# A fixed, hand-made order on all engines for a fused linear-attention and feed-forward kernel, with the v casts on GpSimd

## Chip, cores, metric

One core of a Trainium2 chip. The metric is the device time of one execution in microseconds (us). Span means the stretch that the profile covers; timed runs are about 2 us longer.

## The reference, cut to what matters

```python
# q, k, v: (8 batches, 8 heads, 576 positions, 64)
def phi(x): return np.where(x > 0, x, np.exp(x) - 1.0) + 1.0
q_p, k_p = phi(q), phi(k)
kv  = einsum('bhsd,bhse->bhde', k_p, v);  z = k_p.sum(axis=2)
num = einsum('bhsd,bhde->bhse', q_p, kv)
den = einsum('bhsd,bhd->bhs', q_p, z)[..., None] + 1e-6
x   = (num / den).transpose(0, 2, 1, 3).reshape(4608, 512)
out = (((x @ w1) * (x @ w2)) @ w3) @ w_out       # d_ff 1024
```

## The kernel before

w3 and w_out are fused on the chip into one weight (wf). The tokens are cut into nine chunks of 512 columns. Chunk c needs the attention of batches 0 to c. For each chunk TensorE (PE) runs eight feed-forward groups (F), each of four a_ps and four b_ps matmuls, and four output groups (O). ScalarE (ACT) copies a_ps out of PSUM, where the matmul results stand (its evacuation), VectorE (DVE) multiplies it by b_ps. The attention of a later batch runs beside it: phi of k and q on ACT and DVE, kv, transposes of q (tr), num and den (nd), a logarithm and exponential on ACT as reciprocal, a product on DVE.

Only the weight loads have a fixed order. For all else the framework's scheduler chooses each engine's order; then each engine works its queue in that order and stops at the first instruction that must wait (ScalarE stood so for 14.9 us, as the prediction shows).

```python
def phi_steps(name, b, dst_j, dst_r):
    def ex(j0):
        nc.scalar.activation(out=ev[...], in_=xv[...], func=AF.Exp)
        nc.vector.tensor_scalar_min(out=ev[...], in0=ev[...], scalar1=1.0)
    def st(j):                       # max(x + 1, e): two SBUF inputs
        nc.vector.scalar_tensor_tensor(out=dst_j[...], in0=xv[...], scalar=1.0,
                                       in1=ev[...], op0=ALU.add, op1=ALU.max)
...
def f_unit(c, f):
    a_ps = mm_ps.tile(...); b_ps = mm_ps.tile(...)      # 4 PSUM banks in this pool
    for ps, w in ((a_ps, w1_sb), (b_ps, w2_sb)):
        for kc in range(KC):
            nc.tensor.matmul(ps, w[:, kc, ...], xt[:, kc, cs], ...)
    a_sb = sm.tile(...)
    nc.scalar.copy(out=a_sb, in_=a_ps)
    nc.vector.tensor_mul(out=abs_[c][:, f, :], in0=a_sb, in1=b_ps)
...
k1 = load_qkv("k", k, 1)
after(k1, wl[11])                    # k of batch 1 behind the second w3 block
...                                  # q, v of batch 1; attention of batch 0
for f in range(FC):
    f_unit(0, f)
for i in range(FC):
    wf_unit(i)                       # 8 transposes of w3, copy on ACT, 8 matmuls
run(k_steps(1) + q_steps(1) + v_steps(1))
```

Of the kernel before, what the change touches and what calls it, by code (L numbers as in the profile page):

```python
# [8 lines left out]
F32 = mybir.dt.float32  # L9
BF16 = mybir.dt.bfloat16  # L10
AF = mybir.ActivationFunctionType
ALU = mybir.AluOpType

P = 128
NCH = 512
# [3 lines left out]
def kernel(  # L19
# [11 lines left out]
    nc = tc.nc  # L31
    B, H, S, D = q.shape
# [3 lines left out]
    KC = DM // P  # L36
    FC = DFF // P
    NJ = 4
# [75 lines left out]
    def phi_steps(name, b, dst_j, dst_r):  # L114
        x = raw[name, b]
        e = e_p.tile([P, JW + RW], BF16, tag="e", name="e")
        xv = x[:, 0:JW].rearrange("p (h j d) -> p h j d", h=H, j=NJ)
        ev = e[:, 0:JW].rearrange("p (h j d) -> p h j d", h=H, j=NJ)

        def ex(j0):  # L120
            nc.scalar.activation(out=ev[:, :, j0:j0 + 2, :], in_=xv[:, :, j0:j0 + 2, :], func=AF.Exp)  # L121
            nc.vector.tensor_scalar_min(  # L122
                out=ev[:, :, j0:j0 + 2, :], in0=ev[:, :, j0:j0 + 2, :], scalar1=1.0)

        def exr():
            nc.scalar.activation(out=e[:, JW:], in_=x[:, JW:], func=AF.Exp)
            nc.vector.tensor_scalar_min(out=e[:, JW:], in0=e[:, JW:], scalar1=1.0)

        def st(j):
            nc.vector.scalar_tensor_tensor(  # L130
                out=dst_j[:, j, :].rearrange("p (h d) -> p h d", h=H),
                in0=xv[:, :, j, :], scalar=1.0, in1=ev[:, :, j, :], op0=ALU.add, op1=ALU.max)

        def sr():
            nc.vector.scalar_tensor_tensor(
                out=dst_r, in0=x[:, JW:], scalar=1.0, in1=e[:, JW:],
                op0=ALU.add, op1=ALU.max)

        return [lambda: ex(0), lambda: (st(0), st(1)), lambda: ex(2), lambda: (st(2), st(3)),
                exr, sr]  # L140

    ph = {}

# [9 lines left out]
        ph["q", b] = (qj, qr)  # L153
        return phi_steps("q", b, qj, qr)

    def v_steps(b):
        x = raw["v", b]

        def cj(j0):
            (nc.scalar.copy if b == 0 and j0 == 0 else nc.vector.tensor_copy)(  # L160
                out=vt[:, j0:j0 + 2, :, 0:D],
                in_=x[:, 0:JW].rearrange("p (h j d) -> p j h d", h=H, j=NJ)[:, j0:j0 + 2])

        def cr():
            nc.vector.tensor_copy(
                out=vr[:, :, 0:D], in_=x[:, JW:].rearrange("p (h d) -> p h d", d=D))

        return [lambda: cj(0), lambda: (cj(2), cr())]


    kvz, qts = {}, {}

    def kv_unit(b):
        kj, kr = ph["k", b]
        t = att.tile([P, KC, 2, P], BF16, tag="kvz", name="kvz")
        for g in range(2):
            kvp = at_ps.tile([P, 2, 256], F32, tag="at", name="kvp")
            for hp in (2 * g, 2 * g + 1):
                o = kvp[:, hp % 2, 0:2 * (D + 1)]
# [16 lines left out]
            nc.vector.tensor_tensor(  # L196
                out=tg[:, :, 1, :].rearrange("p a (h e) -> p a h e", h=2),
                in0=src[:, :, :, D:D + 1].to_broadcast([P, 2, 2, D]), in1=mask, op=ALU.mult)
        kvz[b] = t

    def tr_unit(b, part):
        qj, qr = ph["q", b]
        if part == 0:
            qts[b] = att.tile([P, KC, S], BF16, tag="qt", name="qt", bufs=1)
        qt = qts[b]
        if part < 2:
            tp = at_ps.tile([P, KC, 2, P], BF16, tag="at", name="tp")
            for jj in range(2):
                for hp in range(KC):
                    nc.tensor.transpose(  # L210
                        tp[:, hp, jj, :], qj[:, 2 * part + jj, hp * P:(hp + 1) * P], ident)
            nc.vector.tensor_copy(
                out=qt[:, :, part * 256:(part + 1) * 256],
                in_=tp.rearrange("p a j t -> p a (j t)"))
        else:
            for hh in range(2):
                tp = at_ps.tile([P, 2, R], BF16, tag="at", name="tp")
                rows = slice(hh * R, (hh + 1) * R)
                for i in range(2):
                    nc.tensor.transpose(  # L220
                        tp[:, i, :], qr[rows, i * P:(i + 1) * P], ident[rows, rows])
                nc.vector.tensor_copy(out=qt[:, 2 * hh:2 * hh + 2, NJ * P:S], in_=tp)

    def nd_finish(n_ap, d_ap, dst, shape):
        r = lr.tile(shape, F32, tag="lr", name="r")
# [23 lines left out]

    abs_ = {}  # L250

    def f_unit(c, f):
        if f == 0:
            abs_[c] = ab_p.tile([P, FC, NCH], BF16, tag="ab", name="ab")
        cs = slice(c * NCH, (c + 1) * NCH)
        a_ps = mm_ps.tile([P, NCH], F32, tag="mm", name="a_ps")
        b_ps = mm_ps.tile([P, NCH], F32, tag="mm", name="b_ps")
        for ps, w in ((a_ps, w1_sb), (b_ps, w2_sb)):
            for kc in range(KC):
                nc.tensor.matmul(ps, w[:, kc, f * P:(f + 1) * P], xt[:, kc, cs],  # L260
                                 start=(kc == 0), stop=(kc == KC - 1))
        a_sb = sm.tile([P, NCH], F32, tag="a_sb", name="a_sb")
        nc.scalar.copy(out=a_sb, in_=a_ps)  # L263
        nc.vector.tensor_mul(out=abs_[c][:, f, :], in0=a_sb, in1=b_ps)  # L264

    def o_unit(c, m):
        ab = abs_[c]
# [37 lines left out]
        return nc.gpsimd.dma_start(out=t, in_=moe_w3[i * P:(i + 1) * P, :])  # L305


    def wf_unit(i):
        w3b = raw["w3", i]
        tp = at_ps.tile([P, FC, P], BF16, tag="at", name="w3p")  # L310
        for kc in range(FC):
            nc.tensor.transpose(tp[:, kc, :], w3b[:, kc * P:(kc + 1) * P], ident)
        w3t = setup.tile([P, FC, P], BF16, tag="w3t", name="w3t")
        nc.scalar.copy(out=w3t, in_=tp)  # L314
        ps = mm_ps.tile([P, DM], F32, tag="mm", name="wf_ps")
        for kc in range(FC):
            nc.tensor.matmul(ps, w3t[:, kc, :], wo_sb[:, kc, :],  # L317
                             start=(kc == 0), stop=(kc == FC - 1))
        nc.scalar.copy(out=wf_sb[:, i, :], in_=ps)


    def run(steps):
        for s in steps:
            s()

    k0 = load_qkv("k", k, 0)
    q0 = load_qkv("q", q, 0)
    v0 = load_qkv("v", v, 0)
    with tc.manual_schedule(engines={mybir.EngineType.Pool}):
        wl = [i for x in range(4) for i in load_w12(x)]  # L330
        after(wl[0], q0)
        wl += [load_wo(0), load_wo(1)]
        wl += [load_w3(i) for i in range(FC)]
    k1 = load_qkv("k", k, 1)
    after(k1, wl[11])
    load_qkv("q", q, 1)
    load_qkv("v", v, 1)

    run(k_steps(0))
    run(q_steps(0))  # L340
    for p in range(3):
        tr_unit(0, p)
    run(v_steps(0))
    kv_unit(0)
    for hp in range(KC):
        nd_unit(0, hp)
    ndr_unit(0)
    for f in range(FC):
        f_unit(0, f)
    for i in range(FC):  # L350
        wf_unit(i)
    run(k_steps(1) + q_steps(1) + v_steps(1))

    for c in range(1, n_chunks + 1):
        a = c if c == 1 else c + 1
        last = c == n_chunks
        units = []
        if c == 1:
            kv_unit(1)
            for p in range(3):  # L360
                tr_unit(1, p)
            for m in range(4):
                o_unit(0, m)
                nd_unit(1, m)
            ndr_unit(1)
            for n, s in (("k", k), ("v", v), ("q", q)):
                load_qkv(n, s, 2)
            run(k_steps(2) + v_steps(2) + q_steps(2))
        if last:
            for m in range(4):  # L370
                o_unit(c - 1, m)
            break
        a = c + 1
        has = a < B
        if has and a + 1 < B:
            for n, s in (("k", k), ("v", v), ("q", q)):
                load_qkv(n, s, a + 1)
        F = lambda f: (lambda: f_unit(c, f))
        O = lambda m: (lambda: o_unit(c - 1, m)) if c > 1 else (lambda: None)
        KV = lambda: kv_unit(a)  # L380
        T = lambda p: (lambda: tr_unit(a, p))
        N = lambda h: (lambda: nd_unit(a, h))
        NR = lambda: ndr_unit(a)
        if has:
            units = [F(0), KV, F(1), O(0), T(0), T(1), F(2), T(2), O(1), F(3), N(0), F(4), N(1),
                     O(2), F(5), N(2), F(6), N(3), NR, O(3), F(7)]
        else:
            units = [F(0), F(1), O(0), F(2), O(1), F(3), F(4), O(2), F(5), F(6), O(3), F(7)]
        pq = []
        started = 0  # L390
        for i, u in enumerate(units):
            u()
            if has and a + 1 < B:
                if i == 7:
                    pq = k_steps(a + 1) + v_steps(a + 1) + q_steps(a + 1)
                if i >= 7:
                    run(pq[:2] if i > 7 else pq[:1])
                    del pq[:2 if i > 7 else 1]
        run(pq)


# [1 line left out]
_INS = ['q', 'k', 'v', 'moe_w1', 'moe_w2', 'moe_w3', 'moe_w_out']  # L403
# [26 lines left out]
```

## Time and profile before

| | before |
|---|---|
| median time, us | 288.58 (288.14 to 289.36, 3 runs) |
| span of the profiled run | 286.6 |
| last feed-forward group of chunk 0 ends | 53.77 |
| first group of chunk 2 ends | 106.58 |
| last output copy starts | 282.76 |

The rows are moments from the timeline of PE and ACT. The prediction shows the views themselves.

### The profile page before, as it was taken

How to read it: one execution, taken by the hardware profiler on the slowest of the kernel's cores; microseconds unless marked ns; L12 is line 12 of the kernel's file. 1: busy time of each engine (PE TensorE's matmuls, PEld its weight loads, DVE VectorE, ACT ScalarE, POOL GpSimd, SP SyncE). 2: the span in 40 equal slices, each digit the busy share in tenths (PEclk: the TensorE clock that was granted, in tenths of full speed). 3: DMA queues.
4: the chain of work that ended last, by engine and by line, in shares of the span. 5: the costliest groups of instructions: out<-in, count | busy, mean ns of one | idle time of the engine just before them, and what ended most of it. 6: DMA issues, size and time to landing. Idle time of an engine off the chain costs nothing.

```text
span 286.6 us, 3958 instructions
## 1 busy us (share of the span) xinstructions
PE 251.3 (88%) x1413; PEld 122.1 (43%) x1440; DVE 164.4 (57%) x327; ACT 155.2 (54%) x254; POOL 13.6 (5%) x30
## 2 busy tenths in 40 slices
PE   0188605999989999999999999999999999999994
PEld 0043201555535445445544544554455444444441
DVE  0875106913968999965985896498443442221210
ACT  3528007499693992893587279426723763333322
POOL 2472100000000000000000000000000000000000
PEclk9999965999999999999999999999999999999999
DMA  6999999992469881893496081010011111100223
GB/s 209 328 177 202 210 270 352 368 355 79 147 185 279 248 272 27 233 278 116 130 304 210 1 231 46 37 38 37 37 39 54 53 40 40 73 37 37 75 60 123
DMA packets 49715, 43.25 MB, mean 151 GB/s; under 512 B 14368, under 2 KB 44064, under 8 KB 49696
## 3 DMA queue, kind: packets, MB, share of 16 engines
q1 hardware_dynamic: 43264, 37.76, 41.7%
q0 software_dynamic: 6432, 5.24, 11.7%
q8 instruction: 11, 0.18, 0.3%
q14 instruction: 8, 0.07, 0.1%
HBM read 38.80 MB, written 9.44 MB: 168 GB/s over the span
## 4 chain that ended last, share of the span: by engine, by line
PE 72%; DMA 14%; ACT 7%; issue 3%; DVE 2%; POOL 1%; SPq 1%; another core or an unknown queue 0%; ACTq 0%; DVEq 0%
PE a_ps L260 20%; PE b_ps L260 19%; PE o_ps L270 18%; DMA w3b<-in_moe_w_dram 4%; DMA k<-in_k_dram 4%; PE wf_ps L317 4%; PE kvp L181 3%; DMA q<-in_q_dram 3%; DMA w_sb<-in_moe_w_dram 3%; PE tp L210 2%; ACT e L121 2%; PE den L234 2%; PE num L234 2%; PE kvp L187 1%; ACT o_sb L273 1%
## 5 line engine op out<-in xcount | busy, mean ns | idle before, releaser
L260 PEld LDWEIGHTS <-w_sb 128*128 128x128 bf16 x576 | 55.8, 99 | 80.3 <-issue 17.6
L260 PE MATMUL a_ps<-xt,w_sb 128*128 128x512 bf16 x283 | 75.7, 385 | 13.3 <-ACT a_sb L263 12.8
L264 DVE TENSOR_TENSOR ab<-a_sb,b_ps 128x512 bf16<-128x512 f32 x72 | 49.3, 686 | 51.9 <-PE b_ps L260 51.0
L260 PE MATMUL b_ps<-xt,w_sb 128*128 128x512 bf16 x279 | 75.1, 383 | 0.5
L270 PE MATMUL o_ps<-wf_sb,ab 128*128 128x512 bf16 x278 | 65.9, 379 | 0.4
L263 ACT COPY a_sb<-a_ps 128x512 f32<-128x512 f32 x72 | 41.8, 582 | 45.1 <-PE a_ps L260 43.8
L273 ACT COPY o_sb<-o_ps 128x512 f32<-128x512 f32 x36 | 21.1, 585 | 41.9 <-PE o_ps L270 41.4
L270 PEld LDWEIGHTS <-ab 128*128 128x128 bf16 x288 | 27.3, 98 | 31.7
L122 DVE TENSOR_SCALAR e<-e 128x1024 bf16<-128x1024 bf16 x32 | 13.2, 423 | 36.0 <-ACT e L121 35.8
L228 DVE TENSOR_TENSOR xt<-num,r 128x512 bf16<-128x512 f32 (+1 forms) x40 | 24.6, 635 | 15.3 <-ACT r L227 14.8
L226 ACT ACTIVATE r<-den,eps 128x512 f32<-128x512 f32 (+1 forms) x40 | 25.0, 646 | 11.9 <-PE den L234 11.2
L121 ACT ACTIVATE e<-k 128x1024 bf16<-128x1024 f32 x16 | 16.5, 1055 | 20.7 <-DMA k<-in_k_dram 19.1
L227 ACT ACTIVATE r<-r 128x512 f32<-128x512 f32 (+1 forms) x40 | 22.4, 586 | 0.5
L210 PE MATMUL tp<-ident,qj 128*128 128x128 bf16 x128 | 10.1, 230 | 13.6 <-DVE qj L130 13.4
L130 DVE SCALAR_TENSOR_TENSOR kj<-k,e 128x512 bf16<-128x512 f32 x32 | 20.6, 685 | 0.1
L130 DVE SCALAR_TENSOR_TENSOR qj<-q,e 128x512 bf16<-128x512 f32 x32 | 20.4, 685 | 0.0
L121 ACT ACTIVATE e<-q 128x1024 bf16<-128x1024 f32 x16 | 16.6, 1054 | 2.3 <-DMA q<-in_q_dram 2.2
L210 PEld LDWEIGHTS <-qj 128*128 128x128 bf16 x128 | 8.3, 102 | 16.1 <-DVE qj L130 14.2
L317 PE MATMUL wf_ps<-wo_sb,w3t 128*128 128x512 bf16 x61 | 14.2, 380 | 0.7 <-ACT w3t L314 0.5
L181 PE MATMUL kvp<-vt,kj 128*128 128x130 bf16 x128 | 13.9, 232 | 0.9 <-DVE vt L160 0.5
L234 PE MATMUL den<-qt,kvz 128*128 128x512 bf16 x32 | 12.9, 402 | 0.7 <-DVE xt L228 0.7
L234 PE MATMUL num<-qt,kvz 128*128 128x512 bf16 x32 | 12.8, 401 | 0.0
(42 smaller groups left out, 135.0 us busy)
## 6 DMA issues: line engine op xcount, KB each, us to landing
k<-in_k_dram SPq DMA_DIRECT2D x8, 1024.0 KB, 6.8
q<-in_q_dram SPq DMA_DIRECT2D x8, 1024.0 KB, 6.9
v<-in_v_dram SPq DMA_DIRECT2D x8, 1024.0 KB, 7.8
out_dram<-o_sb SPq DMA_DIRECT2D x32, 256.0 KB, 2.3
w_sb<-in_moe_w_dram POOLq DMA_DIRECT2D x8, 256.0 KB, 7.4
w3b<-in_moe_w_dram POOLq DMA_DIRECT2D x8, 256.0 KB, 13.0
k<-in_k_dram SPq DMA_DIRECT2D x16, 64.0 KB, 5.1
q<-in_q_dram SPq DMA_DIRECT2D x16, 64.0 KB, 6.1
```

Source lines behind the costliest of these rows:

```text
L121: nc.scalar.activation(out=ev[:, :, j0:j0 + 2, :], in_=xv[:, :, j0:j0 + 2, :], func=AF.Exp)
L130: nc.vector.scalar_tensor_tensor(out=dst_j[:, j, :].rearrange("p (h d) -> p h d", h=H), in0=xv[:, :, j, :], scalar=1.0, in1=ev[:, :, j, :] ...
L210: nc.tensor.transpose(tp[:, hp, jj, :], qj[:, 2 * part + jj, hp * P:(hp + 1) * P], ident)
L226: nc.scalar.activation(out=r, in_=d_ap, func=AF.Ln, bias=eps[:, 0:1])
L228: nc.vector.tensor_tensor(out=dst, in0=n_ap, in1=r, op=ALU.mult)
L234: nc.tensor.matmul(nd[i], t[:, hp, i, :], qt[:, hp, 0:NJ * P], start=True, stop=True)
L260: nc.tensor.matmul(ps, w[:, kc, f * P:(f + 1) * P], xt[:, kc, cs], start=(kc == 0), stop=(kc == KC - 1))
L263: nc.scalar.copy(out=a_sb, in_=a_ps)
L264: nc.vector.tensor_mul(out=abs_[c][:, f, :], in0=a_sb, in1=b_ps)
L270: nc.tensor.matmul(o_ps, ab[:, f, m * P:(m + 1) * P], wf_sb[:, f, :], start=(f == 0), stop=(f == FC - 1))
L273: nc.scalar.copy(out=o_sb, in_=o_ps)
L317: nc.tensor.matmul(ps, w3t[:, kc, :], wo_sb[:, kc, :], start=(kc == 0), stop=(kc == FC - 1))
```

## The change

The intent: all engines in program order, written so that each feed-forward group carries a share of phi and attention of later batches. Not in the cut: half of the v cast of batch 1 goes to ACT, and w3t gets a third buffer. Core of the diff, cut:

```diff
+        cast = nc.vector.tensor_copy if b == 0 else nc.gpsimd.tensor_copy      # v_unit
...
+        copy = nc.scalar.copy if b == 2 else nc.vector.tensor_copy             # tr_unit
...
-        nc.scalar.copy(out=wf_sb[:, i, :], in_=ps)
+        nc.vector.tensor_copy(out=wf_sb[:, i, :], in_=ps)
...
+    ctx.enter_context(tc.manual_schedule())
...
+    nd_unit(0, 0)
+    nd_unit(0, 1)
+    first = [f_open(0, 0), f_open(0, 1)]
+    for kc in range(KC):
+        for f in range(2):
+            f_mm(0, f, first[f][0], w1_sb, kc)
+            f_mm(0, f, first[f][1], w2_sb, kc)
+        if kc < 2:
+            nd_unit(0, kc + 2)
+        elif kc == 2:
+            ndr_unit(0)
...
+    for f in range(2, FC):
+        if f >= 6:
+            w3_tr(f - 6)
         f_unit(0, f)
...
     for i in range(FC):
+        if i + 2 < FC:
+            w3_tr(i + 2)
+        if i == 2:
+            run(ks, "e0 s0 s1")
+        elif i == 3:
+            run(ks, "e2 s2 s3 eR sR")
...                                  # q in 4 and 5, v in 6
+        wf_mm(i)
...
+        F(0)                        # chunk c, a = c + 1
+        run(qs, "s2 s3 eR sR")
+        K("e0");  kv_unit(a, (0,));  F(1)
+        K("e2");  kv_unit(a, (1,));  O(0)
+        v_unit(a + 1)
+        K("s0 s1 eR");  tr_unit(a, 0);  F(2)
...
```

## The prediction

> **What bounds the kernel now.** I began with the page: TensorE's busy tenths, the granted clock and the DMA share, side by side over the 40 slices of 7.2 us.
>
> ```profile
> PE   0188605999989999999999999999999999999994
> DVE  0875106913968999965985896498443442221210
> ACT  3528007499693992893587279426723763333322
> PEclk9999965999999999999999999999999999999999
> DMA  6999999992469881893496081010011111100223
> ```
>
> From slice 13 on PE has a 9 everywhere. Before that there is a hole in slices 4 to 6, in which the vector and scalar engines are empty too, the clock falls to 6 and 5 tenths, and DMA stays at 9. So there are two regimes. The skill warns that a busy PE is not a PE at its peak, so I then took the busy time by stretches, cut at events that the timeline shows.
>
> ```profile
> 28.10:33.50 5.40, 5.38 (x25) 2.34 (x24) 1.97 (x3) 1.03 (x2) 1.06 (x2) 1.00 1.17 211
> 33.50:46.25 12.75, 0.00 (x1) 0.00 (x0) 0.46 (x2) 1.58 (x3) 0.00 (x0) 0.65 1.10 285
> 46.25:53.77 7.52, 7.30 (x23) 2.90 (x24) 7.52 (x15) 5.35 (x8) 0.00 (x0) 0.68 1.08 349
> 53.77:88.31 34.54, 32.36 (x241) 17.98 (x244) 20.26 (x46) 28.07 (x42) 0.00 (x0) 1.00 0.70 223
> 88.31:106.58 18.27, 18.17 (x102) 8.58 (x102) 18.02 (x38) 13.72 (x23) 0.00 (x0) 1.00 0.83 249
> 106.58:282.80 176.22, 175.05 (x958) 84.21 (x975) 101.08 (x194) 91.37 (x158) 0.00 (x0) 1.00 0.30 95
> ```
>
> The columns are stretch, length, busy us (count) of PE, weight load, DVE, ACT and POOL, then clock, DMA share, GB/s. The timeline shows that a group of four 512-column matmuls starts every 0.86 us when dense: 0.216 us each at clock 1.00. The last stretch runs at that pace: it can't be shortened by an order of instructions. Nothing runs on PE between 33.50 and 46.25, and the next stretch runs three feed-forward groups (24 matmuls, 5.2 us of dense work) in 7.52 us at clock 0.68. Who held PE up, I read from the waits between 30 and 50 us:
>
> ```profile
> DVE e L122 <- ACT e L121: 14.9, 1, 14.9
> ACT e L121 <- DMA k<-in_k_dram: 14.9, 1, 14.9
> PE a_ps L260 <- ACT a_sb L263: 12.8, 1, 12.8
> ```
>
> and from the chain that ended last:
>
> ```profile
> 20.77 12.66 DMA w3b<-in_moe_w_dram
> 33.45 11.20 DMA k<-in_k_dram
> ...
> 44.67 0.02 ACT e L121
> ...
> 45.63 0.57 ACT a_sb L263
> 46.21 0.04 issue
> 46.25 1.86 PE a_ps L260 x4
> ```
>
> This is one inversion in a queue that is served in order. The scheduler put the exponential of k of batch 1 on ScalarE ahead of the evacuation of a finished a_ps. That k is held back on purpose behind the second w3 block, is issued at 33.45 and lands at 44.65. The ready evacuation stands behind it, PE has no free PSUM bank among the four, and feed-forward groups 5, 6 and 7 of chunk 0, whose inputs all lie in SBUF, wait for a transfer that they don't need.
>
> **What the Trainium skill says.** (1) "TensorE: Matmul & The Clock Gate", Part 1, says that an idle TensorE falls to half its clock after some 3.4 us and needs as much busy time to get it back. The trace agrees: after the hole the matmuls stand 0.43 us apart, not 0.216, until about 51 us. (2) "SBUF — State Buffer", Who interferes with whom, says that a GpSimd instruction that reads SBUF and a VectorE instruction with two SBUF inputs, or in a two-port mode, block each other for the whole instruction. The trace before can't show it, GpSimd does only memsets there. (3) "GPSIMD Engine Reference", section 3.1, gives 769 ns for 512 elements in a good one-input loop. From this I estimate 1.5 us for a cast of 1024 columns; no row of this trace has one. (4) "Perfetto Trace Analysis", Optimizing Scalar/DVE Operations, says that a profiled latency overlaps with the next instruction. The trace agrees: four of the 128x512 combines on DVE (685 ns each by the groups) take 2.49 us in a row, so about 0.60 us apart. I count DVE by spacing: 0.60 for 512 columns from PSUM or mixed, 0.34 for the 1024-column minimum, 0.34 for kvz.
>
> **The change part by part.**
>
> *The hole.* With every queue in program order, all eight a_sb copies of chunk 0 and the w3 copies 0 to 4 come before k of batch 1 on ScalarE. Groups 0 to 4 of chunk 0 finish by about 33.5 now; in the new order groups 0 and 1 close at about 28.4 (their inputs take the same path: num and den, logarithm, exponential, product), then six groups of 1.73 us and two blocks of w3 transposes of 0.45 follow: 28.4 + 10.4 + 0.9 = 39.7 us. Before, they ended at 53.77, without these two transposes. So 14.1 us, which are the 12.75 of the hole, 2.3 of low clock (7.52 - 5.2), less 0.9 for transposes done early, give or take 0.1. The blocks of w3 that this needs are there: issued at 19.4 and 20.8, the first by its median of 13 us near 32.4, the second at 33.4 by the chain.
>
> *Does the wait come back?* k of batch 1 still lands near 44.7, q near 47.8 (issued 33.87, longest landing 13.9), v near 50. The fused-weight loop runs from 39.7 for 8 x (1.73 + 0.45), less the two transposes done, plus 1.06 for the q transposes: to about 57.3. Its iteration 2, at about 44, is where ScalarE first asks for k: it waits perhaps nothing, and PE has two fused blocks of slack there, as w3 copies run two ahead. phi of k and q on DVE: per batch 8 x 0.60 + 4 x 0.34 + about 0.9 = 7.1 us, beside 8 fused evacuations at 0.60 newly on DVE, 4.8. I walked both queues: DVE ends this at about 58.9, one to two us behind PE, which the four PSUM banks hold up. No stall over 1 us.
>
> *Until chunk 1 ends.* From 57.3: kv 1.96, four output groups 6.9, four num/den pairs 1.73, the remainder 0.67, makes 11.3; the single num/den slots cost about 1 us in my walk: chunk 1 starts near 69.6. Chunk 1 has 13.8 + 1.96 + 1.06 + 1.73 + 0.67 = 19.2 of PE work without any output group, while DVE has about 17.5 to 18 plus waits for the logarithm and exponential; with 1 to 1.5 us of stalls it ends near 90.3 to 90.7. Before, the same work was done at 106.58. So 16 us, of which 14.1 is the hole and about 2 the 34.54 us stretch (PE busy 32.36).
>
> *Steady stretch.* PE per chunk: 96 x 0.216 + 8 x 0.216 + 1.96 + 1.06 + 0.67 = 26.1 by my sum; the dense trace has 25.8. DVE by spacing: ab 4.8, phi 7.1, kvz 1.4, qt 1.5, xt 2.7 = 17.5. ScalarE, spaced by the same reading (0.48 for an evacuation, 0.96 for an exponential): about 16. Both fit beside 25.8. The v cast that leaves DVE was 2 x 0.60 + 0.2 = 1.4 us, off the path, so it gives nothing directly. Its cost is the lock: cast on GpSimd, 2 x 1.5 + 0.4 = 3.4 us per batch, just when DVE makes k's combine (two SBUF inputs). From F(0) to the first num/den, 9.95 us of PE time, DVE must get through some 9.7 us before qt is complete. Little slack, so the lock shows as 0 to 1 us per chunk, on chunks 2 to 6: I take 0.5, 2.5 us in all. The rest (176.2 us) is as before.
>
> **Sum.** 90.5 + 176.2 + 2.5 + 3.8 (the last copy and output, as before 282.8 to 286.6) = 273.0 of span. Timed runs exceed the span by 2.0 (288.58 - 286.6): 275.0. I put down **274.5 us**, as the middle stretch may have one stall less: a gain of 14.1, 4.9%.
>
> **The rivals.** *The wait moves instead of going.* DMA share is about 1.1 from 28 to 54 us, so the loads are bound there, and k, q, v of batch 1 come no earlier. If ScalarE stands for q or v in the fused loop, copies of w3 stand behind it. For it: the queue is still in order. Against: 17 us of PE work that needs none of it now lies before their use. It would give back 4 to 7 us: 279 to 282. *VectorE becomes the bound.* Page and stretch show DVE busy 18.02 of 18.27 in chunk 1, and a fixed order can't step around a late operand. With the lock at its worst, 1 to 1.5 us in six chunks, and the middle stretch late by 2: 280 to 282. *Everything fits.* PE dense from 28.4 on: 10.4 + 3.6 + 13.8 + 1.06 + 11.3 + 19.2 = 59.4, so 87.8; + 176.2 + 3.8 + 2 = 269.8. *Nothing is gained*, because PE is 88% busy: refuted by the hole, which has no busy PE and no need.
>
> **Range and chances.** 270 to 281: from all fits to one rival in full. Slower than 282.8 would need both the moved wait and the lock. Faster by over 2%: 0.94, within 2%: 0.05, slower: 0.01.
>
> **What would show each step right or wrong.** In the new profile: no PE gap over 2 us from 28 to 90 and clock tenths of 9 there, else the first step fails. The last feed-forward matmul of chunk 0 near 40 us, chunk 1's first near 70 and last near 90. If ScalarE waits for DMA of k, q or v over 2 us while PE idles, the first rival holds. If rows of num/den or tp wait on DVE qt or kj in each chunk, and DVE's combine or minimum is longer than 685 and 423 ns beside GpSimd's casts, the second holds. The cast row itself should read near 1.5 us; at 3 or more the steady stretch loses more. I would be wrong altogether if chunk period on PE rose from 25.8 to over 27.

## The result, and the profile after

Ratios here are the mean time of one kernel's fast runs over that of the other's in the same rounds, so not quite the ratio of the medians quoted.

| | before | after |
|---|---|---|
| median, us | 288.36 | 279.73 (279.05 to 280.77, 4 runs) |
| ratio | | 0.9705 (0.9657 to 0.9753) |
| span | 286.6 | 277.9 |
| groups 0 and 1 of chunk 0 done (start of group 2) | 28.1 | 32.1 |
| last group of chunk 0 done | 53.77 | 43.37, two w3 transpose blocks (0.9 us) done as well |
| first matmul of chunk 1 | 88.31, kv and 7 transposes of the next batch done as well | 75.55 |
| first group of chunk 2 done | 106.58 | 98.09 |
| last output copy starts | 282.76 | 274.06 |

The predicted 274.5 was too low by 5.2 us; the measured time lies inside the range. The gain is 8.6 us where 14.1 was expected. The page's 40 slices after:

```profile
PE   0078899989798999999999999999999999999994
DVE  0773533795898787759666966786574442232210
PEclk9999999999999999999999999999999999999999
DMA  7999999999189935675455663011001200111122
```

The hole of slices 4 to 6 is gone, in PE and in the clock. In its place are shallow dips up to slice 12. The busy time by stretch (length, PE, weight load, DVE, ACT, POOL, clock, DMA share, GB/s), cut at the moments of the table:

```profile
28.10:43.37 15.27, 14.34 (x84) 6.91 (x83) 6.31 (x10) 8.52 (x14) 1.06 (x2) 1.00 1.13 237
43.37:75.55 32.18, 28.68 (x199) 15.45 (x201) 23.34 (x46) 21.25 (x30) 3.95 (x5) 1.00 0.88 284
75.55:98.09 22.54, 20.84 (x125) 10.47 (x128) 18.61 (x37) 19.10 (x33) 4.01 (x3) 1.00 0.91 277
98.09:274.10 176.01, 174.88 (x958) 84.57 (x975) 100.48 (x189) 95.20 (x162) 12.08 (x12) 1.00 0.32 100
```

The last stretch is 176.01 us against 176.22 before: nothing won and nothing lost. What PE waited for between 28 and 100 us (us in total, times, longest):

```profile
PE num L240 <- DVE xt L234: 1.5, 2, 1.2
PE a_ps L264 <- DVE xt L234: 1.5, 2, 0.9
PE kvp L187 <- DVE qt L218: 1.3, 1, 1.3
PE den L240 <- ACT qt L218: 0.9, 1, 0.9
```

One wait of 12.8 us has become several of about 1 us, mostly on DVE. And PE's timeline in the head, as I call all that comes before group 2 of chunk 0 (start, duration, operation):

```profile
24.16 0.58 PE L264 MATMUL a_ps<-xt,w_sb 128*128 128x512 bf16 x1 [0.94 <-DVE xt L234]
24.54 0.63 PE L264 MATMUL b_ps<-xt,w_sb 128*128 128x512 bf16 x1
24.97 0.63 PE L264 MATMUL a_ps<-xt,w_sb 128*128 128x512 bf16 x1
...
28.38 0.52 PE L240 MATMUL den<-qt,kvz 128*128 128x512 bf16 x1
28.74 0.38 PE L240 MATMUL num<-qt,kvz 128*128 128x512 bf16 x1
28.96 0.38 PE L264 MATMUL a_ps<-xt,w_sb 128*128 128x512 bf16 x1
```

Up to 28.4 the matmuls stand 0.43 us apart, then 0.22: half speed until then, although the clock row reads 9 for these slices. In the kernel before, the last matmul at that pace starts at about 22 us. The head of this trace also began its kv matmuls 0.8 us later than in the kernel before (17.04 against 16.28), so not all of the delay is clock.

### The profile page after: what moved, and what is told of

The parts are those of the page before. It is cut to its first block, busy times and chain, and to the rows that moved or that the text cites. A ratio compares the mean times of both kernels' runs of the same rounds, so it can differ in the third digit from the quotient of the medians.

```text
span 277.9 us, 3982 instructions
## 1 busy us (share of the span) xinstructions
PE 250.3 (90%) x1413; PEld 122.7 (44%) x1440; DVE 162.2 (58%) x310; ACT 155.4 (56%) x251; POOL 33.8 (12%) x50
## 3 DMA queue, kind: packets, MB, share of 16 engines
q0 software_dynamic: 6432, 5.24, 12.1%
## 4 chain that ended last, share of the span: by engine, by line
PE 75%; DMA 10%; ACT 4%; DVE 4%; POOL 3%; issue 2%; SPq 2%; ACTq 0%; DVEq 0%
PE o_ps L283 21%; PE a_ps L264 21%; PE b_ps L264 21%; DMA w3b<-in_moe_w_dram 5%; DMA q<-in_q_dram 3%; PE kvp L187 3%; POOL w_sb L306 2%; DMA k<-in_k_dram 2%; PE tp L216 2%; PE num L240 2%; PE den L240 2%; SPq L106 2%; PE kvp L193 1%; DVE wf_sb L337 1%; ACT r L232 1%
## 5 line engine op out<-in xcount | busy, mean ns | idle before, releaser
L264 PE MATMUL a_ps<-xt,w_sb 128*128 128x512 bf16 x270 | 74.6, 383 | 3.6 <-DVE xt L234 2.4
L283 PE MATMUL o_ps<-wf_sb,ab 128*128 128x512 bf16 x286 | 67.2, 379 | 0.2 <-issue 0.2
L234 DVE TENSOR_TENSOR xt<-num,r 128x512 bf16<-128x512 f32 (+1 forms) x40 | 25.5, 638 | 29.5 <-ACT r L233 29.3
L162 POOL CAST vt<-v 128x1024 bf16<-128x1024 f32 x13 | 15.6, 1228 | 130.5 <-PE kvp L187 91.8
L232 ACT ACTIVATE r<-den,eps 128x512 f32<-128x512 f32 (+1 forms) x40 | 25.8, 645 | 9.5 <-PE den L240 9.4
L233 ACT ACTIVATE r<-r 128x512 f32<-128x512 f32 (+1 forms) x40 | 23.5, 587 | 1.3
L216 PE MATMUL tp<-ident,qj 128*128 128x128 bf16 x128 | 11.0, 230 | 13.9 <-DVE qj L131 13.9
L123 DVE TENSOR_SCALAR e<-e 128x1024 bf16<-128x1024 bf16 x32 | 14.7, 461 | 14.2 <-ACT e L121 14.2
L131 DVE SCALAR_TENSOR_TENSOR kj<-k,e 128x512 bf16<-128x512 f32 x32 | 22.5, 732 | 0.2
L131 DVE SCALAR_TENSOR_TENSOR qj<-q,e 128x512 bf16<-128x512 f32 x32 | 21.0, 685 | 0.2
```

What stands on the lines that cost most here:

```text
L131: nc.vector.scalar_tensor_tensor(out=dst_j[:, j, :].rearrange("p (h d) -> p h d", h=H), in0=xv[:, :, j, :], scalar=1.0, in1=ev[:, :, j, :] ...
L216: nc.tensor.transpose(tp[:, hp, jj, :], qj[:, 2 * part + jj, hp * P:(hp + 1) * P], ident)
L232: nc.scalar.activation(out=r, in_=d_ap, func=AF.Ln, bias=eps[:, 0:1])
L233: nc.scalar.activation(out=r, in_=r, func=AF.Exp, scale=-1.0)
L234: nc.vector.tensor_tensor(out=dst, in0=n_ap, in1=r, op=ALU.mult)
L264: nc.tensor.matmul(ps, w[:, kc, f * P:(f + 1) * P], xt[:, kc, c * NCH:(c + 1) * NCH], start=(kc == 0), stop=(kc == KC - 1))
```

## The experiments

Ten runs were made, in three sets, each set with the kernel before in the same rounds. All gave correct results. Two questions: is the inversion the whole cause of the gain, and where did the rest of the expected gain go?

### Only the inversion taken away

The kernel before, scheduler and all, with a scheduling dependency (no semaphore) added by the helper that it already has:

```diff
-            nc.scalar.activation(out=ev[...], in_=xv[...], func=AF.Exp)
+            ins = nc.scalar.activation(out=ev[...], in_=xv[...], func=AF.Exp)
+            if b == 1:
+                after(ins, hold[0])
```

In a_late, hold[0] is the last a_ps copy of chunk 0; in a_late2, the fourth w3 copy.

> The kernel before, automatic order kept, with one scheduling dependency more: the exponentials of batch 1 come on ScalarE after the last a_ps evacuation of chunk 0. Theory (the one inversion on ScalarE is the whole gain, and the hand-made order adds nothing, rather gives some back): the PE hole of 12.8 us and the low clock after it go, but the exponential of k now stands in front of the third w3 copy and waits there for k, which lands near 45: 275 to 278 us. Rival (the gain of the change comes from the new order as a whole, the greedy order finds another wait of the same length elsewhere): 285 us or more.

> As the run before, but the exponentials of batch 1 come after the fourth w3 copy of the fused-weight loop, by when k has landed. Theory: 273 to 276 us, faster than the hand-made order (279.7), no PE gap over 2 us between 24 and 88 us, chunk 0's last group done near 39 us. Rival: 279 us or more, because work is only pushed to a later stretch where VectorE is full.

Measured: a_late 282.21 us, ratio 0.9799 (0.9765 to 0.9834); a_late2 280.51, ratio 0.9733 (0.9673 to 0.9793). Both are slower than the theory said, and a_late2 falls into the rival's range. Its profile says why. The chain that ended last, from 33 to 60 us, and one row of DVE's timeline:

```profile
46.20 5.23 DMA v<-in_v_dram
...
51.64 0.69 DVE vt L163
52.33 0.60 DVE ab L267
52.93 0.04 issue
52.98 5.70 PE wf_ps L322 x16
```

```profile
51.03 1.30 DVE L163 CAST vt<-v 128x1024 bf16<-128x1024 f32 x2 [13.31 <-DMA v<-in_v_dram]
```

The scheduler had put the v cast of batch 1 on DVE ahead of the product (ab) of the last group. DVE stood 13.3 us for v, PE lost 6.0 us and then ran at a low clock. It is the same kind of inversion in a second queue, but not one that the first had covered: in the kernel before, the cast stands behind that product.

```profile
54.04 0.69 DVE L264 TENSOR_TENSOR ab<-a_sb,b_ps 128x512 bf16<-128x512 f32 x1
55.59 1.29 DVE L160 CAST vt<-v 128x1024 bf16<-128x1024 f32 x2
```

The scheduler made it when the exponentials were held back. (a_late lost 5.7 us to a w3 copy behind the waiting exponential, as expected; its DVE stood for v too, 12.2 us.) So a third version, a_late3, also puts the v casts of batch 1 behind the last combine of q:

```diff
+            if b == 1:
+                after(ins, qlast[0])        # at the three v casts
```

> As a_late2 (exponentials of batch 1 after the fourth w3 copy), and also the v casts of batch 1 on VectorE after the last combine of q of batch 1. In a_late2 the greedy order had put a v cast, whose load lands at 51 us, in front of the product of group 7: PE lost 6.0 us there and ran at low clock after it. Theory (the inversions in the queues are the whole loss, and the greedy order is otherwise as good or better than the hand-made one): 272 to 275 us, 5 to 7 us under the changed kernel. Rival (freed here, the time is lost to VectorE later): 278 us or more.

Measured: 276.84 us (275.88 to 278.36), ratio 0.9593 (0.955 to 0.9637). That is short of the theory's 272 to 275, but clearly faster than the changed kernel, whose ratio in a second set below is 0.9684 (0.9664 to 0.9704). Busy time by stretch:

```profile
28.10:38.50 10.40, 10.35 (x49) 4.71 (x49) 4.72 (x7) 3.96 (x7) 1.06 (x2) 1.00 1.14 209
38.50:75.04 36.54, 32.85 (x241) 18.14 (x243) 24.38 (x53) 30.00 (x45) 0.00 (x0) 1.00 0.99 318
```

Chunk 0's last group ends at 38.50: 15.3 us earlier than before. From there to the end of chunk 2's first group (93.75) it takes 55.25 us where the kernel before took 52.81: 2.4 us are given back, 1.6 of them in one wait of a fused-weight matmul for a w3 copy. The rest is kept: the span is 274.1.

### The inversion put back alone

The changed kernel, with the first exponential of k of batch 1 moved up, and with it the minimum that follows it on DVE (both are in step e0; the rest of the edit only makes the steps earlier):

```diff
     for f in range(2, FC):
+        if f == 3:
+            run(ks, "e0")
         if f >= 6:
```

> The changed kernel with the inversion put back alone: the first exponential of k of batch 1 goes to ScalarE just before the a_ps evacuation of group 3 of chunk 0. Theory: PE stops with its four PSUM banks full near 36 to 37 us and until k lands near 45, a hole of 8 to 9 us, then low clock for about 2 us: 289 to 291 us against 279.7. Rival (the inversion is not what cost the time in the kernel before): 280 to 282 us.

Measured: 290.13 us (289.6 to 291.6), ratio 1.0079 (1.0038 to 1.0121). The waits between 30 and 50 us are of the same kind as in the kernel before, up to 3 us shorter:

```profile
DVE e L123 <- ACT e L121: 12.0, 1, 12.0
ACT e L121 <- DMA k<-in_k_dram: 12.0, 1, 12.0
PE a_ps L264 <- ACT a_sb L269: 9.9, 1, 9.9
```

One exponential and its minimum, too early in their queues, cost about 10 us, more than the whole change gains. In the kernel before, too, the minimum stood ahead of ready products on DVE; whether one of the two queues alone would do the harm was not tested. With a_late3 this settles the first question: the gain is the inversion; the rest of the hand-made order, taken as a whole, adds nothing to it.

### The v casts back on VectorE

```diff
-        cast = nc.vector.tensor_copy if b == 0 else nc.gpsimd.tensor_copy
+        cast = nc.vector.tensor_copy
```

> The changed kernel with the v casts of batches 1 to 7 back on VectorE (the first half of batch 1 stays on ScalarE). My prediction charged the GpSimd casts 2.5 us for the shared lock; the trace of the changed kernel shows no PE stall in the steady stretch, so the lock should be worth nothing there. Theory: 279 to 280.5 us, the same within 0.5%, as 1.4 us of DVE per batch fit in the slack. Rival (GpSimd casts give VectorE needed room in chunk 1 and in the fused loop): 281 to 283 us. Rival (the lock does cost): 276 to 278 us.

Measured: 282.75 us (281.21 to 283.3), ratio 0.9806 (0.9766 to 0.9847), so about 3 us slower than the changed kernel (other rounds than its 0.9705). My theory of "the same" is wrong; the rival that GpSimd gives VectorE needed room holds. PE's waits in the whole run:

```profile
PE a_ps L264 <- DVE xt L234: 3.2, 4, 1.6
PE kvp L187 <- DVE qt L218: 2.1, 2, 1.7
PE den L240 <- DVE qt L218: 1.4, 4, 0.3
```

The third line is the steady stretch: once in each of chunks 2 to 5, den waits for the copy of the transposed q. The first output group of a chunk starts every 26.32 us (103.42, 129.74) against 25.82 in the changed kernel (101.78, 127.60): 0.5 us per chunk. The rest, 1.6 us, is lost before chunk 2, although this trace's head was done 2.0 us earlier (30.16 against 32.12). Casts and what they met, in the changed kernel (duration in ns, least, median, most):

```profile
L162 POOL CAST vt<-v x13: 1038/1044/2687, 52.1 to 180.1; 128x1024 bf16<-128x1024 f32 x13
L131 DVE SCALAR_TENSOR_TENSOR kj<-k,e x32: 679/685/879, 7.9 to 185.5; 128x512 bf16<-128x512 f32 x32
L123 DVE TENSOR_SCALAR e<-e x32: 416/427/676, 7.4 to 198.8; 128x1024 bf16<-128x1024 bf16 x32
```

The two engines do get in each other's way. The longest stretch is GpSimd's (up to 2.69 us for a cast of 1.04); VectorE's combines grow from 0.68 to at most 0.88, its minimum from 0.43 to at most 0.68. In a steady chunk (from 102 us) the lengthened minimum and two lengthened combines cost DVE about 0.24 + 0.37 = 0.6 us, against 1.4 (the prediction's estimate) for doing the casts itself. GpSimd's casts there take 3.07 us, 0.6 more than the shortest (2.03 + 0.40).

### The low clock in the head

Matmuls on constants, whose result nobody reads, keep PE busy in its idle time of the head:

```diff
+    wtile = mm_ps.tile([P, NCH], F32, tag="mm", name="warm")
+    def warm(n):
+        for _ in range(n):
+            nc.tensor.matmul(wtile, ident, wsrc, start=True, stop=True)
     run(k_steps(0), ALL)
     run(q_steps(0), ALL)
+    warm(36)
     for p in range(3):
         tr_unit(0, p)
+        warm((4, 1, 3)[p])
...
     nd_unit(0, 1)
+    warm(3)
```

> The changed kernel with matmuls on constants, whose result nobody reads, put into the idle stretches of PE before and between the head's work (36 before the first transposes, 8 among them, 3 before the first feed-forward groups). Theory (the 3.7 us by which chunk 0's first groups closed late are mostly the low clock: the matmuls up to 28.4 us stood 0.43 us apart): groups 0 and 1 close at 28 to 29 instead of 32.1 and the time is 275.5 to 277.5. Rival (the chain den, logarithm, exponential, product sets the pace and the clock is beside it): 279 to 280.

Measured: 277.0 us (three runs at 276.9 to 277.1, one at 279.6), ratio 0.9616 (0.9566 to 0.9667). In its trace the head runs at full speed (these lines against 24.16 to 24.54 above), and group 2 starts at 28.67 instead of 32.12:

```profile
22.65 0.38 PE L266 MATMUL a_ps<-xt,w_sb 128*128 128x512 bf16 x1 [0.66 <-DVE xt L236]
22.86 0.38 PE L266 MATMUL b_ps<-xt,w_sb 128*128 128x512 bf16 x1
```

The theory holds: the low clock costs the changed kernel 2 to 3 us (2.0 and 2.6 by its two ratios, 2.7 between the medians; the intervals of the ratios just overlap). Chunk 0's last group now ends at 39.92.

### Phi of batch 1 earlier

```diff
-        if i == 2:
+        if i == 1:
             run(ks, "e0 s0 s1")
```

and so on for the other parts, the v cast in iteration 5 instead of 6.

> The changed kernel with the phi of batch 1 and its v cast one iteration earlier in the fused-weight loop (iterations 1 to 5 instead of 2 to 6). Theory (VectorE is idle until 50 us and then two us behind PE, because the order starts phi late; the 1.25 us in which kv waits for the qt copy, and part of later waits, come from that): 277.5 to 279. Rival (k has not landed in iteration 1, ScalarE stands for it and the w3 copies behind it): 280 to 282.

Measured: 277.75 us (276.07 to 278.83), ratio 0.9632 (0.9593 to 0.9672). The kv wait shrinks from 1.25 to 0.43 us. But this profile alone can't carry the point: in it, the clock of the unaltered head rose by luck at about 21.8 us, and its kv matmuls began 0.8 us earlier; the two together moved everything by 2.7.

### The changed kernel again, and the two best versions

g_hand is e_warm and f_mid together. g_auto is a_late3 with constant matmuls at the same places of its head (without the last three).

> The changed kernel again, unaltered, to have it in the same rounds as the next two and a second trace of its head. Theory (the moment at which the clock rises is not fixed by the program: with the same head the traces show it at 28.4, 27.6 and 25.9 us, and 21.8 in the run with phi moved earlier): 278.5 to 280.5 us, and chunk 0's groups 0 and 1 close anywhere from 28.5 to 32.5. Rival (the clock always rises late in this kernel): 32 us again.

> The changed kernel with both mends: the matmuls on constants in the head and phi of batch 1 one iteration earlier. If the two losses are separate terms they add up: 274.5 to 276 us, 4 to 5 under the changed kernel. If the mended head only moves everything against the landing of k, iteration 1 now asks for k at about 42 us and ScalarE waits some 2 us for it: 276.5 to 278.

> The kernel before with automatic order, the dependencies of a_late3, and the matmuls on constants in the head. The head of the kernel before gets its clock by about 24 us (22 in a_late3's trace), so less is to be had than in the changed kernel: 275 to 276.5 us, 0.5 to 1.5 under a_late3's 276.8. If the gain of the constant matmuls in the changed kernel came from something other than the clock: 276.8 or more.

| label | median, us | ratio to before, same rounds |
|---|---|---|
| after_r | 279.74 (279.33 to 280.82) | 0.9684 (0.9664 to 0.9704) |
| g_hand | 276.22 (275.72 to 276.64) | 0.9562 (0.9542 to 0.9582) |
| g_auto | 275.52 (274.77 to 278.71) | 0.9558 (0.9519 to 0.9596) |

The changed kernel repeats. Its clock rose late again (28.5 us; groups closed at 31.9), so the five traces of this head without constant matmuls (after, b_inv, c_vdve, f_mid, after_r) have it at 28.4, 28.0, 25.6, 21.8 and 28.5 us, each time the start of the first shortened matmul; the 27.6 of the expectation was misread. In the four traces of the scheduler's head (before, a_late, a_late2, a_late3) it came between 21 and 24 us. So the hand-made head goes with the late clock in four of five; what in it sets the moment is not settled.

The two mends together give 0.9684 to 0.9562, 3.5 us; g_hand lies between the two expected ranges. Its trace speaks against the second guess (k asked for too early): ScalarE waits only 0.6 us for k of batch 1, PE never for a w3 copy, and the kv wait is 0.4 us where e_warm has 1.6. g_hand and g_auto can't be told apart, and g_auto's gain over a_late3 (0.9593, other rounds) is within the intervals. Both are faster than before and than the changed kernel.

g_auto's traced run is its slowest (278.71 us): there PE waited 2.05 us for a product on DVE at 70 us, and its 512-column matmuls still stood 0.43 us apart at 78 us. No longer idle time precedes this low clock, so 2.05 us seem to have been enough, less than the 3.4 us that the prediction took from the Trainium skill ("TensorE: Matmul & The Clock Gate", Part 1); after waits of 1.26 us in a_late3 and in the kernel before the matmuls kept their pace.

## Why the prediction was partly right and partly wrong

**The inversion: right.** The hole came from one exponential ahead of a ready evacuation: a_late3 takes it away (and keeps the scheduler from making another on VectorE) and wins, b_inv brings it back and loses. Its size was fair too: in a_late3, where the head is the old one, chunk 0's end moved by 15.3 us, against 15.0 foreseen (14.1, and 0.9 for two transpose blocks that only the hand-made order does before).

**"Groups 0 and 1 close at about 28.4 (their inputs take the same path)": this step failed.** They closed at 32.1, and chunk 0's last group at 43.37 where I had 39.7: 3.7 us. I took the head's clock for granted. Half speed until 28.4 us is most of it, as e_warm shows: at full speed chunk 0's last group ended at 39.92. The hand-made head lets PE idle 0.94 us before its first feed-forward matmul; the scheduler's head has a similar gap, 0.66, after six num and den matmuls instead of four, and ran at full speed after it. This is the largest mis-sized term.

**The wait does not come back: right.** In the fused loop, which now runs later, ScalarE and VectorE wait for no k, q or v of batch 1; the 4.3 us that ScalarE waits for k in the whole run are those at the start. The first rival is refuted.

**"No stall over 1 us" up to chunk 1: failed, by 2.3 us.** From chunk 0's end to chunk 1's start I had 29.9 us (39.7 to 69.6); it took 32.18. VectorE, little used up to 50 us because the order starts phi in iteration 2, is late afterwards: kv waits 1.25 us for a qt copy and num 1.2 for a product. An earlier start takes most of the kv wait away (1.3, 1.6 and 1.6 us in after, after_r and e_warm; 0.4 in f_mid and g_hand). In time it is not clear of noise: f_mid's interval meets the changed kernel's, g_hand's that of e_warm; the ratios of these two differ by about 1.6 us, their medians by 0.8.

**"Before, the same work was done at 106.58": an error of counting.** That stretch of the kernel before holds nine groups, eight of chunk 1 and the first of chunk 2; I set it against eight. The moment to compare was 104.86, so I credited 1.7 us too much. Chunk 1 itself took 20.8 us (75.55 to 96.37), against the 20.9 that I went on with (69.6 to 90.5). That was luck in part: the terms as given, 19.2 and 1 to 1.5 of stalls, end it at 89.8 to 90.3, not at 90.3 to 90.7. (Another slip, without consequence: in the kernel before GpSimd does not do only memsets, it also spends 12.1 of its 13.6 busy us on issuing the weight loads.)

**The lock, 2.5 us: wrong in size and, as a verdict on the part, in sign.** The pairs of casts do collide, but the slack that I had worked out (9.7 us of DVE work in a window of 9.95) just held, and the steady stretch lost nothing. I had called the cast's removal from DVE worthless because it was off the path. c_vdve shows that it was the slack itself: without it each steady chunk loses 0.5 us. My estimate of the cast, 1.5 us, was high; undisturbed it takes 1.04.

The sum closes: 3.7 + 2.3 + 1.7 for the three misses, less 2.5 for the lock, is 5.2, and the span is 277.9 against my 273.0; of the 0.3 left over, 0.2 are the steady stretch (176.01 for 176.2). **What became of the expected gain**: 3.7 us were lost in the head, 1.7 were never there, and 2.3 went into waits, mostly for VectorE, before chunk 2; the 2.5 set aside for the lock were not spent. That the errors partly cancel is luck.

## What to carry to other kernels

When a tuned kernel has one large hole, look in each in-order queue for the instruction that waits for a late load ahead of one that is ready, and first try to move that instruction alone: here a few scheduling dependencies did better than the rewritten order of every engine, and no worse than that order with both mends. Then look at all queues again, since the scheduler answered the first mend with a new inversion in another queue. And when an order is laid by hand, the head needs its own check: spacing of the matmuls, not the clock row, tells whether PE is at full speed.

## What the Trainium skill lacked or had wrong

- "TensorE: Matmul & The Clock Gate", Part 1, speaks of a warm-up of about 3.4 us and says that its moment varies by about half a microsecond with a free-running window. In five executions of one head, PE at work from about 13 us with gaps of up to about 1 us, full speed came between 21.8 and 28.5 us, and group 2 started between 29.4 and 32.1. The clock row of the profile read 9 tenths all that time while the matmuls stood 0.43 us apart, so it doesn't show the first warm-up; that Part does warn that the clock events of a trace can be unreliable.
- "SBUF — State Buffer", Who interferes with whom, says that the loser of the shared port blocks fully and that issue order decides who that is. The runs agree that instructions of both engines stretch; the page has no figure for this mix: a GpSimd cast went from 1.04 to up to 2.69 us, a VectorE combine from 0.68 to at most 0.88 us, each engine lost about 0.6 us per steady chunk, and the move to GpSimd still gained 0.5 us per chunk.
- No page that I read has the case that decided here: a scheduler's order that puts an instruction with a late load ahead of a ready one, at 12.8 us of PE idle, and that makes a new one in another queue, at 6.0 us, once the first is held back.
